# A loading stage reordered, a PSUM place alternated and DMA transposes moved to mid-batch in an attention and gated-FFN kernel

## The chip, the cores and the metric

The kernel runs on one core of a Trainium2 chip. The metric is the device time of one execution in microseconds; a profiled span is about 1.8 us shorter than the time of the same execution. In this text PE is TensorE, DVE is VectorE, ACT is ScalarE, POOL is GpSimd and SP is the engine whose queue issues most DMAs (72 of the 86 issues that the old kernel's DMA view lists). "Granted clock" is the TensorE clock that the profile records as granted, as a share of full speed.

Ratios are computed as the mean time of one kernel's fast runs over the mean of the other kernel's fast runs in the same rounds, so they are not quite the ratio of the medians quoted beside them. Each experiment was timed against the old kernel in the same rounds; medians of different groups of rounds differ by up to 1.4 us for the old kernel itself (259.6 to 261.0), so across groups the ratios are the better guide.

## The reference

For each of 8 batches and 8 heads, a cross attention in both directions between x (512 rows of 64) and a state (32 rows of 64); then a gated feed-forward layer over all rows.

```python
scores = scale * x @ state^T;  a  = softmax(scores);  xread = a @ state      # 512 rows per head
scores2 = scale * state @ x^T; a2 = softmax(scores2); sread = a2 @ x         # 32 rows per head
t = concat(xread, sread) over rows, heads side by side                        # (8 * 544, 512)
out = (sigmoid(t @ w_gate) * (t @ w_val)) @ w_out                             # d_ff = 1536
```

## The kernel before

PSUM holds the buffers that this kernel's matmuls write to; an eviction is the copy of a result out of such a buffer, here by ACT or DVE (a 128x512 copy of SW took 0.59 us on ACT and 0.68 us on DVE in the old kernel).

The kernel never forms xread. It multiplies the state with the gate and value weights first (SW, "visits"), and the attention a^T (aT) is then the moving operand of the gate/value matmuls. For one batch there are 12 gate/value steps `gv`, each four 128x512 matmuls, then 12 output steps `out_mm` of four. Batch b's output steps run one batch behind, woven into batch b+1's loop, together with the attention of the batch after that (nb).

```python
def at_xT_dma(b):                       # x^T by four DMA transposes on SP's queue
    for c in range(4):
        nc.sync.dma_start_transpose(xT[:, :, c], xbs[b][:, c]...)

def at_S(b, i, place):                  # scores, then E = exp on ACT
    for jj in range(2):
        for c in range(4):
            nc.tensor.matmul(ps[...], xTs[b][:, 2*i+jj, c], sTz[:, b, 2*i+jj], ...)
    nc.scalar.activation(E1s[b]..., ps..., AF.Exp, scale=scale)

def at_norm(b, i, eng):                 # rs = row sums, ri = 1/rs, ab = E * ri
    nc.vector.tensor_reduce(rs, E, AX.X, ALU.add)
    nc.vector.reciprocal(ri, rs)
    eng.tensor_tensor(abs_[b]..., E, ri.unsqueeze(3).to_broadcast(...), ALU.mult)

def gv(b, f, place=None):               # two PSUM buffers, one tanh on ACT, one multiply on DVE
    # (four matmuls, cut)
    nc.scalar.activation(th, pss[0], AF.Tanh, scale=0.5)
    nc.vector.scalar_tensor_tensor(glus[b][:, f], th, 1.0, pss[1], ALU.add, ALU.mult)

def out_mm(b, k):                       # row block c = k // 3, a third of its 12 matmuls
    if f0 == 0:
        ops[b, c] = p_out.tile(...) if b < B else p_sw.tile(...)   # p_out holds ONE buffer
    # (four matmuls; after the last third: copy by ACT, then the store on SP's queue)
```

The loading order: state and x of batch 0 on SP's queue; on POOL's queue the first 256 columns of both weights, x of batch 1, the rest of the weights, x of batch 2, and later w_out. The loop, cut to what the argument needs:

```python
for b in range(1, B + 1):
    for f in range(12):
        out_mm(b - 1, f)                          # for b > 1 also gv(b, f)
        if f == 0:
            if b > 1: at_xT_dma(nb)               # transposes of nb = b + 1
            load_x(nb + 1, nc.sync)
        elif f == 2: at_S(nb, 0, AT)              # needs the transposes
        elif f == 3: at_S(nb, 1, AT)              # AT: one PSUM buffer
        elif f == 4: at_norm(nb, 0, nc.vector); at_Eb(nb)   # Eb: casts of E on POOL
        elif f == 5: at_norm(nb, 1, nc.vector)
        elif f == 7: at_aT(nb, AT, (vec,))
        elif f == 8: at_sr(nb, AT)
        if f == 11: cast_x(nb + 1, pool, 0, 4); cast_x(nb + 1, pool, 4, 4)
```

The softmax here doesn't subtract the row's maximum and nothing guards it: scores larger than these inputs give would overflow.

## Time and profile before

The old kernel takes 260.53 us (median of 4 runs, 259.14 to 261.48). Three markers in the trace cut its span into stages: the first output matmul, the first gate/value step of batch 2, and the last output copy of batch 6.

| stage | from, us | to, us | length, us |
|---|---|---|---|
| loading, batches 0 and 1 | 0 | 57.75 | 57.75 |
| batch 1 of the loop (output of batch 0) | 57.75 | 75.25 | 17.50 |
| batches 2 to 6 | 75.25 | 205.73 | 130.48 |
| the rest | 205.73 | 257.9 | 52.17 |

The page of the old kernel has the span in 40 slices of 6.4 us; each digit is a share in tenths, PE's busy share and then its granted clock.

```profile
span 257.9 us, 4608 instructions
...
PE   7677499899887999899989998999899999999994
...
PEclk9959769999999999999999999999999999999999
```

PE looks busy nearly everywhere, but the clock falls to 5, 7 and 6 tenths in slices of the loading stage. The timeline of the old kernel's PE shows what goes before the last of these falls. The columns are start, length, what, and in brackets the idle time before it and what ended it.

```profile
26.57 0.62 PE L171 MATMUL swp<-wv,sTz 64*32 64x512 bf16 x8
29.82 1.03 PE L139 MATMUL aTp<-ident,ab 128*128 128x128 bf16 x8 [2.64 <-DVE ab L132]
32.03 4.36 PE L207 MATMUL gvp<-aT,SW 128*128 128x512 bf16 x10 [1.18 <-DVE aT L143]
```

After 2.64 us of idleness the eight small transposes take 1.03 us, and ten gate/value matmuls take 4.36 us, some 430 ns each against 216 at a full clock (0.86 us from one step of four to the next, 77.64 to 78.50 to 79.36 us). The granted clock was 0.50 from 30 to 35 us.

The waits of the old kernel's PE over the whole span (total, times, longest):

```profile
PE Sp L115 <- DMA xT<-xb: 5.5, 7, 1.1
PE aTp L139 <- DVE ab L132: 2.6, 1, 2.6
PE outp L228 <- ACT res L232: 1.9, 3, 0.7
```

The chain that ended last, on the page, by engine and by line:

```profile
PE 58%; DVE 11%; SPq 9%; DMA 7%; ACT 6%; issue 5%; POOL 1%; ACTq 0%; DVEq 0%; POOLq 0%
PE outp L228 24%; PE gvp L207 22%; SPq L107 8%; DMA xT<-xb 5%; DVE glu L215 4%; PE gvp L210 4%; PE swp L171 3%; ACT th L214 2%; DVE rs L129 2%; ACT res L232 2%; DMA xf<-in_x_dram 2%; PE Sp L115 2%; PE aTp L139 1%; PE srp L152 1%; ACT SW L193 1%
```

The issue of the transposes (L107) and their flight (xT) are on the chain with 13%. That is not what can be saved: during most of it PE has other work. The saving is what PE waits, and the timeline of batch 2 shows it:

```profile
74.88 5.97 SPq L107 DMA_TRANSPOSE xT<-xb  x4
...
80.23 0.22 PE L115 MATMUL Sp<-sTz,xT 128*128 128x64 bf16 x2
...
80.81 0.20 PE L115 MATMUL Sp<-sTz,xT 128*128 128x64 bf16 x1 [0.37 <-DMA xT<-xb]
...
82.12 0.32 PE L115 MATMUL Sp<-sTz,xT 128*128 128x64 bf16 x5 [1.11 <-DMA xT<-xb]
82.28 1.03 PE L228 MATMUL outp<-wo,glu 128*128 128x512 bf16 x4
```

The four transposes occupy SP's queue for 5.97 us from step 0 on, each lands 2.5 us after its issue (median of the 24 in the trace, 2.4 to 6.0), and PE arrives at the scores of step 2 after 5.35 us. Eight score matmuls that wait for nothing take 0.23 us (the next eight, at 84.17, in the chain); here the next output matmul starts 2.05 us after the first of the eight.

### The profile page before, as it was taken

What the parts mean: (1) busy time and instruction counts of PE and PEld (TensorE: products, weight loads), DVE (VectorE), ACT (ScalarE), POOL (GpSimd) and SP (SyncE); (2) the same over time, 40 slices, a digit from 0 to 9 for tenths busy, and PEclk for the clock granted to TensorE, in tenths of its full rate; (3) what the DMA queues carried; (4) which work ended last, traced back from release to release, by engine and by line L of the source; (5) the groups of instructions that cost most, each with busy time, mean ns of one, the idle gap of its engine ahead of it and who ended that gap; (6) DMA issues with size and microseconds to landing.
All of it is one profiled execution on the core that took longest, in us unless ns stands there. A gap on an engine that the chain in (4) does not pass through costs nothing.

```text
span 257.9 us, 4608 instructions
## 1 busy us (share of the span) xinstructions
PE 232.3 (90%) x1816; PEld 116.0 (45%) x1816; DVE 120.5 (47%) x201; ACT 140.8 (55%) x262; POOL 41.1 (16%) x71
## 2 busy tenths in 40 slices
PE   7677499899887999899989998999899999999994
PEld 7434233343433454444434443444344544466643
DVE  3714945773332664376535653565337543332210
ACT  3557347675645756675567556765556554433311
POOL 4974220000500600050005000500020000000000
PEclk9959769999999999999999999999999999999999
DMA  7999999001144511551165105610511111111103
GB/s 236 180 234 206 283 189 226 3 0 43 41 103 100 206 43 56 103 211 41 39 100 194 68 22 128 192 66 21 119 41 42 43 66 56 43 41 57 67 21 101
DMA packets 30965, 25.98 MB, mean 101 GB/s; under 512 B 14048, under 2 KB 26080, under 8 KB 30944
## 3 DMA queue, kind: packets, MB, share of 16 engines
q1 hardware_dynamic: 24448, 18.75, 25.6%
q0 software_dynamic: 6352, 6.82, 14.1%
q8 instruction: 14, 0.23, 0.3%
q10 hardware_dynamic: 144, 0.13, 0.1%
q14 instruction: 7, 0.06, 0.1%
HBM read 18.35 MB, written 8.91 MB: 106 GB/s over the span
## 4 chain that ended last, share of the span: by engine, by line
PE 58%; DVE 11%; SPq 9%; DMA 7%; ACT 6%; issue 5%; POOL 1%; ACTq 0%; DVEq 0%; POOLq 0%
PE outp L228 24%; PE gvp L207 22%; SPq L107 8%; DMA xT<-xb 5%; DVE glu L215 4%; PE gvp L210 4%; PE swp L171 3%; ACT th L214 2%; DVE rs L129 2%; ACT res L232 2%; DMA xf<-in_x_dram 2%; PE Sp L115 2%; PE aTp L139 1%; PE srp L152 1%; ACT SW L193 1%
## 5 line engine op out<-in xcount | busy, mean ns | idle before, releaser
L215 DVE SCALAR_TENSOR_TENSOR glu<-th,gvp 128x512 bf16<-128x512 f32 (+1 forms) x108 | 70.9, 658 | 105.5 <-ACT th L214 73.8
L207 PE MATMUL gvp<-aT,SW 128*128 128x512 bf16 x384 | 100.9, 389 | 5.8 <-DVE aT L143 1.7
L228 PE MATMUL outp<-wo,glu 128*128 128x512 bf16 x396 | 100.3, 379 | 1.9 <-ACT res L232 1.9
L214 ACT ACTIVATE th<-gvp 128x512 f32<-128x512 f32 (+1 forms) x108 | 61.8, 573 | 65.2 <-PE gvp L207 54.3
L207 PEld LDWEIGHTS <-SW 128*128 128x128 bf16 x384 | 38.1, 100 | 54.7 <-issue 13.0
L228 PEld LDWEIGHTS <-glu 128*128 128x128 bf16 x396 | 36.3, 98 | 43.5 <-issue 7.4
L193 ACT CAST SW<-swp 128x512 bf16<-128x512 f32 x92 | 52.5, 588 | 6.2 <-PE swp L171 5.4
L122 POOL CAST Eb<-E 128x256 bf16<-128x256 f32 x32 | 11.9, 415 | 140.4 <-ACT E L116 140.4
L232 ACT ACTIVATE res<-outp 128x512 f32<-128x512 f32 x33 | 19.7, 597 | 26.5 <-PE outp L228 24.1
L86 POOL CAST xb<-xf 128x1024 bf16<-128x1024 f32 x14 | 16.0, 1172 | 7.2 <-DMA xf<-in_x_dram 6.5
L116 ACT ACTIVATE E<-Sp 128x512 f32<-128x512 f32 x16 | 9.6, 608 | 6.4 <-PE Sp L115 6.4
L115 PE MATMUL Sp<-sTz,xT 128*128 128x64 bf16 x128 | 7.5, 194 | 6.2 <-DMA xT<-xb 5.5
L171 PE MATMUL swp<-wv,sTz 64*32 64x512 bf16 (+1 forms) x208 | 11.0, 365 | 2.2 <-DMA wv<-in_moe_w_val_dram 1.5
L129 DVE TENSOR_REDUCE rs<-E 128x16 f32<-128x512 f32 x16 | 10.9, 679 | 4.2 <-ACT E L116 4.2
L132 DVE TENSOR_TENSOR ab<-E,ri 128x512 bf16<-128x512 f32 x15 | 11.6, 774 | 0.5
L115 PEld LDWEIGHTS <-xT 128*128 128x128 bf16 x128 | 6.1, 98 | 10.5 <-DMA xT<-xb 6.3
L171 PEld LDWEIGHTS <-sTz 64*32 64x32 bf16 x416 | 4.4, 89 | 13.2 <-issue 12.4
L171 PE MATMUL swp<-wg,sTz 64*32 64x512 bf16 (+1 forms) x208 | 10.1, 370 | 0.0
L158 DVE RECIPROCAL r<-srp 128x128 f32<-128x128 f32 x8 | 7.7, 956 | 4.9 <-PE srp L155 4.9
L139 PE MATMUL aTp<-ident,ab 128*128 128x128 bf16 x64 | 5.7, 241 | 3.5 <-DVE ab L132 2.6
L263 PE MATMUL warm<-ident 128*128 128x128 bf16 x68 | 6.9, 280 | 1.4 <-POOL ident masks.py:199 1.4
L143 DVE COPY aT<-aTp 128x1024 bf16<-128x1024 bf16 (+1 forms) x8 | 5.2, 653 | 5.5 <-PE aTp L139 5.5
(47 smaller groups left out, 102.5 us busy)
## 6 DMA issues: line engine op xcount, KB each, us to landing
out_dram<-res SPq DMA_DIRECT2D x31, 256.0 KB, 2.3
xf<-in_x_dram SPq DMA_DIRECT2D x5, 1024.0 KB, 5.9
xf<-in_x_dram POOLq DMA_DIRECT2D x2, 1024.0 KB, 14.1
wo<-in_moe_w_out_dram POOLq DMA_DIRECT2D x3, 512.0 KB, 16.2
xf<-in_x_dram SPq DMA_DIRECT2D x2, 512.0 KB, 5.1
wg<-in_moe_w_gate_dram POOLq DMA_DIRECT2D x2, 512.0 KB, 13.5
wv<-in_moe_w_val_dram POOLq DMA_DIRECT2D x2, 512.0 KB, 15.3
sf<-in_state_dram SPq DMA_DIRECT2D x1, 512.0 KB, 3.6
```

The lines of the kernel that those rows point to most:

```text
L86: cp(xbs[b].rearrange("p c h d -> p h c d")[:, lo:lo + n], xfs[b][:, lo:lo + n])
L107: nc.sync.dma_start_transpose(xT[:, :, c], xbs[b][:, c].rearrange("p h d -> p (h d)"))
L115: nc.tensor.matmul(ps[:, c, :, jj], xTs[b][:, 2 * i + jj, c], sTz[:, b, 2 * i + jj], start=True, stop=True)
L122: nc.gpsimd.tensor_copy(Ebs[b][:, c], E1s[b][:, c])
L129: nc.vector.tensor_reduce(rs, E, AX.X, ALU.add)
L171: nc.tensor.matmul(pss[e][j * Ns:(j + 1) * Ns, o:o + n], sTz[rows, b, j, e], (wg, wv)[w][rows, j, lo:lo + n], start=True, stop=True)
L193: cp(*sw_left.pop(0))
L207: nc.tensor.matmul(ps, SWs[b][:, g, w, fs], aTs[b][:, g], start=(g == 0), stop=(g == 1))
L214: nc.scalar.activation(th, pss[0], AF.Tanh, scale=0.5)
L215: nc.vector.scalar_tensor_tensor(glus[b][:, f], th, 1.0, pss[1], ALU.add, ALU.mult)
L228: nc.tensor.matmul(ops[b, c], glus[b][:, f, c * 128:(c + 1) * 128], wo[:, f], start=(f == 0), stop=(f == NF - 1))
L232: nc.scalar.activation(res, ops[b, c], AF.Copy, scale=0.5)
```

## The change

The intent: x of batches 0 and 1 ahead of all weights, so that both attentions are done by the time the first weights land; then one list of gate/value steps and visits, with evictions shared evenly between ACT and DVE; two PSUM places for the row blocks of batch 0's output; and in the loop the casts of x at step 5 and the transposes at step 7, for the next batch but one, in place of step 11 and step 0. The diff, cut to its core:

```diff
 def out_mm(b, k):
-            ops[b, c] = (p_out.tile(...) if b < B else p_sw.tile(...))
+            place = SWP if b == B else GV if b == 0 and c % 2 else OU
+            ops[b, c] = place[0].tile((128, 512), FP, name="outp", tag=place[1])
 ...
     load_x(0, nc.sync, 2)
+    load_x(1, nc.sync)
 ...
-    load_w(0, 256)
-    load_x(1, nc.gpsimd)
-    load_w(256, 256)
-    load_w(512, 512)
-    ...                                  # attention 0, then gv, visits and attention 1 mixed by hand
+    at_xT_pe(0, 0, AT, (vec,))           # attention 0
+    ...
+    load_w(0, 256)
+    ...
+    at_norm(0, 1, nc.vector)
+    load_w(256, 256)
+    cast_x(1, pool, 4, 4)
+    ...                                  # other weights, x of batch 2, w_out
+    warm(32, SWP)                        # 32 dummy matmuls
+    at_xT_pe(1, 0, OU, (act,))           # attention 1
+    at_aT(0, AT, (vec, act))
+    at_xT_pe(1, 1, OU, (vec,))
+    warm(8, SWP)
+    ...                                  # first visit, scores of batch 1, gv(0, 0), gv(0, 1)
+    sT_copy(0, slice(2, B), act)         # transposed state of batches 2 to 7, on ACT
+    at_norm(1, 0, nc.vector)
+    sT_copy(1, slice(2, B), act)
+    at_norm(1, 1, nc.vector)
+    order = [(sw_visit, 1, 0, 256), (sw_visit, 0, 256, 256), (gv, 0, 2), (at_aT, 1, AT, (vec,)), (gv, 0, 3), ...]
+    for fn, *args in order:
+        ...
+        fn(*args)
+        sw_evac(act, vec)
 ...
                 if f == 0:
-                    if b > 1:
-                        at_xT_dma(nb)
                     if nb + 1 < B:
                         load_x(nb + 1, nc.sync)
 ...
                 elif f == 5:
                     at_norm(nb, 1, nc.vector)
+                    if nb + 1 < B:
+                        cast_x(nb + 1, pool, 0, 4)
+                        cast_x(nb + 1, pool, 4, 4)
                 elif f == 7:
                     at_aT(nb, AT, (vec,))
+                    if nb + 1 < B:
+                        at_xT_dma(nb + 1)
 ...
-                if nb + 1 < B and f == 11:
-                    cast_x(nb + 1, pool, 0, 4)
-                    cast_x(nb + 1, pool, 4, 4)
```

More of the change, by code (lines that the diff above doesn't have):

```diff
@@ L60 @@
     XS = wp.tile((128, 4, B * Ns), BF, name="XS")
+    AT, OU, GV, SWP = (p_at, "at"), (p_out, "outp"), (p_gv, "gv"), (p_sw, "swp")
     xfs, xbs, xTs = {}, {}, {}
@@ L172, in sw_mm, with sw_visit @@
                                  (wg, wv)[w][rows, j, lo:lo + n], start=True, stop=True)
-    def sw_visit(b, lo, n):
+    def sw_visit(b, lo, n, *ws):
         if b not in SWs:
             SWs[b] = fp.tile((128, 2, 2, dff), BF, name="SW", bufs=2)
-        if n == 256:
+        if not ws:
             pss = [p_sw.tile((128, 512), FP, name="swp", tag="swp") for e in range(2)]
@@ L182, in sw_visit @@
                 sw_left.append((SWs[b][:, e, :, lo:lo + n], pss[e].rearrange("p (w n) -> p w n", w=2)))
-        else:
-            for w in range(2):
-                pss = [p_sw.tile((128, 512), FP, name="swp", tag="swp") for e in range(2)]
-                sw_mm(pss, b, w, lo, n, 0)
-                for e in range(2):
-                    sw_left.append((SWs[b][:, e, w, lo:lo + n], pss[e]))
+        for w in ws:
+            pss = [p_sw.tile((128, 512), FP, name="swp", tag="swp")[:, :n] for e in range(2)]
+            sw_mm(pss, b, w, lo, n, 0)
+            for e in range(2):
+                sw_left.append((SWs[b][:, e, w, lo:lo + n], pss[e]))
     def sw_evac(*cps):
@@ L224, in out_mm @@
         if f0 == 0:
-            ops[b, c] = (p_out.tile((128, 512), FP, name="outp", tag="outp") if b < B
-                         else p_sw.tile((128, 512), FP, name="outp", tag="swp"))
+            place = SWP if b == B else GV if b == 0 and c % 2 else OU
+            ops[b, c] = place[0].tile((128, 512), FP, name="outp", tag=place[1])
         for f in range(f0, f0 + 4):
@@ L254, in out_last, with warm @@
                 nc.sync.dma_start(rows_of(b, c)[:, cs], res[:, cs])
-    AT, OU, GV, SWP = (p_at, "at"), (p_out, "outp"), (p_gv, "gv"), (p_sw, "swp")
-    def warm(n):
-        ps = p_gv.tile((128, 512), FP, name="warm", tag="gv")
+    def warm(n, place):
+        ps = place[0].tile((128, 512), FP, name="warm", tag=place[1])
         for _ in range(n):
@@ L274 @@
     nc.scalar.activation(pre, ident[:, 0:1], AF.Exp)
-    warm(36)
+    warm(36, SWP)
     sb = wp.tile((128, 16, 2, D), BF, name="sb")
     nc.vector.tensor_copy(sb[:, :, 0], sf)
-    nc.scalar.copy(sb[:, 0:12, 1], sf[:, 0:12])
-    nc.gpsimd.tensor_copy(sb[:, 12:16, 1], sf[:, 12:16])
-    load_w(0, 256)
-    load_x(1, nc.gpsimd)
-    load_w(256, 256)
-    load_w(512, 512)
-    load_w(1024, 512)
-    load_x(2, nc.gpsimd)
-    cast_x(0, vec, 0, 4)
+    nc.scalar.copy(sb[:, :, 1], sf)
+    cast_x(0, vec, 0, 2)
+    cast_x(0, act, 2, 2)
     stp = []
     for i in range(2):
-        ps = p_sw.tile((128, 8, 128), BF, name="stp", tag="swp")
+        ps = p_gv.tile((128, 8, 128), BF, name="stp", tag="gv")
         for l in range(8):
@@ L302, in sT_copy @@
             cp(dst, src.rearrange("p b j u l -> p (b j) u l"))
-    sT_copy(0, slice(0, 1), vec)
-    sT_copy(1, slice(0, 1), act)
     at_xT_pe(0, 0, AT, (vec,))
+    sT_copy(0, slice(0, 2), vec)
+    sT_copy(1, slice(0, 2), act)
+    cast_x(0, pool, 6, 2)
     cast_x(0, act, 4, 2)
-    cast_x(0, vec, 6, 2)
-    warm(8)
+    load_w(0, 256)
+    warm(4, SWP)
     at_S(0, 0, OU)
-    at_xT_pe(0, 1, AT, (vec,))
-    at_norm(0, 0, nc.gpsimd)
-    warm(8)
-    at_S(0, 1, GV)
-    sT_copy(0, slice(1, B), act)
@@ L316 @@
-    at_norm(0, 1, nc.vector)
-    warm(8)
-    sw_visit(0, 0, 256)
-    sw_evac(act, act)
-    warm(8)
-    at_aT(0, AT, (vec, act))
-    sT_copy(1, slice(1, B), act)
-    cast_x(1, pool, 0, 4)
+    at_xT_pe(0, 1, SWP, (vec, act))
+    at_norm(0, 0, nc.vector)
+    at_S(0, 1, SWP)
+    cast_x(1, act, 0, 4)
+    at_norm(0, 1, nc.vector)
+    load_w(256, 256)
     cast_x(1, pool, 4, 4)
-    at_Eb(0)
+    load_w(512, 512)
+    load_w(1024, 512)
+    load_x(2, nc.gpsimd)
     for q in range(3):
         load_wo(q)
-    gv(0, 0)
@@ L331 @@
-    gv(0, 1, SWP)
-    at_xT_pe(1, 0, AT, (vec,))
-    at_xT_pe(1, 1, OU, (act,))
-    sw_visit(0, 256, 256)
-    sw_evac(act, vec)
-    sw_visit(1, 0, 256)
-    gv(0, 2)
-    sw_evac(act, act)
-    at_S(1, 0, AT)
-    at_S(1, 1, OU)
-    gv(0, 3, SWP)
-    sw_visit(1, 256, 256)
+    warm(32, SWP)
[3 more added lines that the diff above has]
+    warm(8, SWP)
+    sw_visit(0, 0, 256, 0)
+    sw_evac(act, vec)
+    at_S(1, 0, AT)
+    sw_visit(0, 0, 256, 1)
@@ L343 @@
+    sw_evac(act, vec)
+    gv(0, 0, SWP)
+    at_S(1, 1, OU)
+    gv(0, 1, SWP)
+    sT_copy(0, slice(2, B), act)
     at_norm(1, 0, nc.vector)
+    sT_copy(1, slice(2, B), act)
     at_norm(1, 1, nc.vector)
+    at_Eb(0)
     at_Eb(1)
-    sw_evac(act, act)
-    at_sr(0, OU)
-    sw_visit(0, 512, 512)
-    sw_evac(act, act, act)
-    at_aT(1, AT, (vec,))
-    sw_evac(vec)
-    gv(1, 0)
-    gv(1, 1, SWP)
-    gv(0, 4)
-    gv(1, 2, SWP)
-    sw_visit(1, 512, 512)
-    sw_evac(act, act)
-    gv(1, 3)
@@ L359 @@
-    sw_evac(act, act)
-    gv(0, 5, SWP)
-    gv(0, 6)
-    gv(1, 4, SWP)
-    gv(1, 5)
-    gv(0, 7, SWP)
-    sw_visit(0, 1024, 512)
-    sw_evac(act, vec)
-    gv(1, 6)
-    sw_evac(act, act)
-    gv(1, 7, SWP)
-    at_sr(1, OU)
-    gv(0, 8)
-    sw_visit(1, 1024, 512)
-    sw_evac(act, vec)
-    gv(0, 9, SWP)
-    sw_evac(act, act)
+    order = [(sw_visit, 1, 0, 256), (sw_visit, 0, 256, 256), (gv, 0, 2), (at_aT, 1, AT, (vec,)), (gv, 0, 3),
+             (sw_visit, 1, 256, 256), (gv, 1, 0), (gv, 1, 1), (gv, 1, 2),
+             (sw_visit, 0, 512, 512, 0), (gv, 1, 3), (sw_visit, 0, 512, 512, 1), (at_sr, 0, OU), (gv, 0, 4),
+             (sw_visit, 1, 512, 512, 0), (gv, 0, 5), (sw_visit, 1, 512, 512, 1), (gv, 0, 6), (gv, 0, 7), (gv, 1, 4),
+             (gv, 1, 5), (sw_visit, 0, 1024, 512, 0), (gv, 1, 6), (sw_visit, 0, 1024, 512, 1), (gv, 1, 7),
+             (at_sr, 1, OU), (gv, 0, 8), (sw_visit, 1, 1024, 512, 0), (gv, 0, 9), (sw_visit, 1, 1024, 512, 1),
+             (gv, 0, 10), (gv, 0, 11), (gv, 1, 8), (gv, 1, 9), (gv, 1, 10), (gv, 1, 11)]
@@ L376 @@
+    n_gv = 0
+    for fn, *args in order:
+        if fn is gv:
+            args.append(SWP if n_gv % 2 else GV)
+            n_gv += 1
+        fn(*args)
+        sw_evac(act, vec)
     cast_x(2, pool, 0, 4)
@@ L378 @@
     at_xT_dma(2)
-    gv(0, 10)
-    gv(0, 11, SWP)
-    for f in range(8, NF):
-        gv(1, f, SWP if f % 2 else GV)
     for b in range(1, B + 1):
@@ L393 @@
                 if f % 4 == 0:
-                    sw_visit(nb, f * 128, 512)
+                    sw_visit(nb, f * 128, 512, 0, 1)
                 sw_evac(act)
                 if f == 0:
-                    if b > 1:
-                        at_xT_dma(nb)
                     if nb + 1 < B:
```

## The prediction

> **What bounds the kernel now** (chain of waits, timeline, windows).
>
> 1. Loading, 0 to 57.8 us (first output matmul at 57.75). The stage holds 24 gate/value steps of four 128x512 matmuls. A step takes 0.86 us when nothing waits, so they need 20.7 us; from the first at 16.1 us they take 41.7. TensorE's granted clock is 0.59 at 15 to 20 us and 0.50 at 30 to 35 us, after idle stretches (2.6 us at 29.8 before the transpose of batch 1's attention). Eight matmuls there take 3.44 us, 430 ns each, against 216 warm. [...] ACT carries most evictions (0.59 us per 128x512), in clumps, while DVE idles.
> 2. Batch 1 of the loop, 57.8 to 74.4 us: one output PSUM buffer, so the next row block waits for ACT's copy. Waits: 1.9 us in three, plus drains, about 2.3 us.
> 3. Batches 2 to 6, periods 25.8 to 26.7 us: DMA transposes are issued at step 0 (four of 1.2 to 2.1 us on the queue, then 2.5 us to landing), and scores need them at step 2. Waits charge 5.5 us to this; from the score matmuls' ideal end to the next output matmul I count 1.8, 0.9, 1.3, 0.9 and 1.9: 6.8 us.
> 4. After 206 us all is PE-bound at 1.73 us per pair, and unchanged.
>
> **What changes.**
> - Stage 3: casts at step 5, transposes at step 7, some 8 us before their use. All 6.8 us lie on the critical path. In the old trace the casts already run at steps 4 to 5 (87.07 us), because POOL waits for x, so no new collision with DVE. I allow 0.5 us for new waits: gain 6.3 us.
> - Stage 2: output blocks alternate two pools: gain 2.3 us.
> - Stage 1: x of batch 1 puts about 3 us of DMA (x of batch 0 landed 2.9 us after state) ahead of the first weights, whose issue also moves from 5.3 to about 8 us. Both attentions fill that gap, with dummy matmuls keeping the clock. First gate/value step at 16 to 17.5 us, no earlier than now. After it DVE owes 24 x 0.69 + 11 evictions x 0.68 + normalisation of batch 1 3.3 + state read 3.1 + one copy 0.7, or 31 us; ACT about 24; PE about 26. DVE becomes the limit. At 88% use (guess) the stage ends 35 us later, near 52 us: gain about 5.5 us, the least certain term. The last weight chunk should land near 32 us and be needed near 38.
>
> Sum: 14.1 us. I take 13.4, allowing for small new waits: 260.4 - 13.4 = 247.0 us, 243 to 252.
>
> **What would show it.** First output matmul at 50 to 54 us; granted clock at least 0.95 from 16 us on; DVE over 80% busy from 17 to 50 us. No PE wait on the DMA transpose, periods of batches 2 to 6 near 24.9 us. No wait of output matmuls on ACT's copy in batch 1, which lasts about 14.2 us.
>
> **What would make it wrong.** Weights landing later than 15.5 us, or a chunk arriving after its visit (waits on weight DMA); TensorE falling cold again; DVE's order stalling PE in the loading stage (gate/value matmuls waiting on DVE), leaving its end near 55 us; transposes holding the issue queue at step 7 and delaying output stores; with the transpose wait gone, gate/value steps waiting for DVE at steps 4 to 6, 0.5 us or more per batch.
>
> Chances: faster by over 2% 0.92, within 2% 0.07, slower 0.01.

## The result

The new kernel takes 247.88 us (median of 4 runs, 247.49 to 248.67). The ratio to the old one is 0.9522, with a 95% interval of 0.9473 to 0.9572.

| stage | before, us | after, us | gain, us | predicted gain, us |
|---|---|---|---|---|
| loading | 57.75 | 53.01 | 4.74 | 5.5 |
| batch 1 | 17.50 | 15.76 | 1.74 | 2.3 |
| batches 2 to 6 | 130.48 | 125.11 | 5.37 | 6.3 |
| the rest | 52.17 | 52.22 | -0.05 | 0 |

The markers after are 53.01, 68.77, 193.88 and 246.1 us. The gains of the two profiles add up to 11.8 us, where the medians differ by 12.65; the experiment on the loading stage shows where the rest probably lies. The page of the new kernel, slices of 6.2 us:

```profile
span 246.1 us, 4632 instructions
...
PE   7674999999999999999999999999999999999993
...
PEclk9998699999999999999999999999999999999999
```

One deep dent of the clock is left (8 and 6 tenths, 18 to 31 us). The chain that ended last has no transposes on it any more:

```profile
PE 76%; DVE 13%; issue 4%; ACT 4%; DMA 2%; SPq 0%; ACTq 0%; DVEq 0%
```

The longest waits of the new kernel's PE, and the one that is new in batch 1:

```profile
PE gvp L208 <- DVE glu L216: 2.5, 9, 0.3
PE gvp L208 <- ACT SW L194: 2.0, 2, 1.8
PE gvp L208 <- DVE SW L194: 1.6, 1, 1.6
...
PE Sp L116 <- ACT E L117: 0.6, 1, 0.6
```

The waits for the transposes (5.5 us) and for ACT's output copy (1.9 us) are gone. The last line came in their place. In batch 1 the steps are short, because there are no gate/value steps yet. The second score matmuls now arrive before ACT has emptied the one buffer that both use.

The transposes of batch 4, in the new kernel's timeline:

```profile
80.62 5.12 SPq L108 DMA_TRANSPOSE xT<-xb  x4
...
99.18 0.40 PE L116 MATMUL Sp<-sTz,xT 128*128 128x64 bf16 x8
99.42 1.03 PE L229 MATMUL outp<-wo,glu 128*128 128x512 bf16 x4
```

They are issued 18.6 us before the scores that use them; the eight score matmuls run together, and the output matmul follows 0.24 us after their start (2.05 us in batch 2 before).

The loading stage is less clean. In the new kernel's timeline between 19 and 29 us, ACT and DVE have older work in front of the evictions (SW) that the third gate/value step waits for:

```profile
19.57 1.92 ACT L296 COPY sTz<-stp 64x384 bf16<-64x384 bf16 x4
...
22.64 0.61 PE L208 MATMUL gvp<-aT,SW 128*128 128x512 bf16 x1 [1.78 <-ACT SW L194]
...
23.54 1.28 DVE L194 CAST SW<-swp 128x512 bf16<-128x512 f32 x2
24.88 1.46 PE L208 MATMUL gvp<-aT,SW 128*128 128x512 bf16 x3 [1.62 <-DVE SW L194]
...
26.98 1.91 PE L208 MATMUL gvp<-aT,SW 128*128 128x512 bf16 x4
```

The windows view of the same stretch (window and length, busy us and number of instructions of each engine, granted clock, DMA share, GB/s):

```profile
20.00:25.00 5.00, 1.14 (x17) 0.37 (x17) 4.68 (x9) 2.53 (x6) 2.27 (x6) 0.74 1.24 207
25.00:30.00 5.00, 5.00 (x34) 2.07 (x34) 2.37 (x4) 1.71 (x4) 0.00 (x0) 0.58 1.13 301
```

PE worked 1.14 of 5 us, the clock fell (0.74, then 0.58), and the next four matmuls took 1.91 us in place of 1.03.

### The profile page after: what moved, and what is told of

Read it like the earlier page. It is cut to its first block, busy times and chain, and to the rows that moved or that the text cites. A ratio compares the mean times of both kernels' runs of the same rounds, so it can differ in the third digit from the quotient of the medians.

```text
span 246.1 us, 4632 instructions
## 1 busy us (share of the span) xinstructions
PE 229.8 (93%) x1828; PEld 114.4 (46%) x1828; DVE 128.4 (52%) x210; ACT 139.2 (57%) x258; POOL 36.4 (15%) x68
## 4 chain that ended last, share of the span: by engine, by line
PE 76%; DVE 13%; issue 4%; ACT 4%; DMA 2%; SPq 0%; ACTq 0%; DVEq 0%
PE outp L229 30%; PE gvp L208 29%; PE swp L172 5%; DVE glu L216 4%; PE gvp L211 4%; DVE rs L130 3%; DVE ab L133 3%; PE srp L153 2%; PE aTp L140 2%; ACT th L215 2%; DMA sf<-in_state_dram 2%; PE srp L156 2%; DVE ri L132 1%; PE Sp L116 1%; ACT E L117 1%
## 5 line engine op out<-in xcount | busy, mean ns | idle before, releaser
L208 PEld LDWEIGHTS <-SW 128*128 128x128 bf16 x384 | 36.7, 98 | 53.1 <-issue 7.9
L194 ACT CAST SW<-swp 128x512 bf16<-128x512 f32 (+1 forms) x85 | 48.7, 581 | 7.9 <-PE swp L172 7.1
L87 POOL CAST xb<-xf 128x1024 bf16<-128x1024 f32 (+1 forms) x14 | 14.3, 1045 | 19.0 <-PE srp L156 13.0
L133 DVE TENSOR_TENSOR ab<-E,ri 128x512 bf16<-128x512 f32 x16 | 15.8, 989 | 0.5
L172 PE MATMUL swp<-wg,sTz 64*32 64x512 bf16 (+1 forms) x208 | 10.6, 374 | 0.5 <-DVE glu L216 0.5
L116 PE MATMUL Sp<-sTz,xT 128*128 128x64 bf16 x128 | 6.5, 193 | 2.5 <-DVE sTz L296 1.1
L194 DVE CAST SW<-swp 128x512 bf16<-128x512 f32 (+1 forms) x13 | 8.3, 643 | 0.3 <-PE swp L172 0.2
L211 PE MATMUL gvp<-XS,wv 128*128 128x256 bf16 x48 | 7.2, 272 | 0.1
## 6 DMA issues: line engine op xcount, KB each, us to landing
wv<-in_moe_w_val_dram POOLq DMA_DIRECT2D x2, 512.0 KB, 11.8
```

The costliest lines, as they stand in the source:

```text
L87: cp(xbs[b].rearrange("p c h d -> p h c d")[:, lo:lo + n], xfs[b][:, lo:lo + n])
L116: nc.tensor.matmul(ps[:, c, :, jj], xTs[b][:, 2 * i + jj, c], sTz[:, b, 2 * i + jj], start=True, stop=True)
L133: eng.tensor_tensor(abs_[b].rearrange("p c e (j n) -> p (c e) j n", n=Ns)[:, :, 2 * i:2 * i + 2], E, ri.unsqueeze(3).to_broadcast((128, 8, ...
L172: nc.tensor.matmul(pss[e][j * Ns:(j + 1) * Ns, o:o + n], sTz[rows, b, j, e], (wg, wv)[w][rows, j, lo:lo + n], start=True, stop=True)
L194: cp(*sw_left.pop(0))
L208: nc.tensor.matmul(ps, SWs[b][:, g, w, fs], aTs[b][:, g], start=(g == 0), stop=(g == 1))
```

## The experiments

Twelve kernels were run, all with correct results, each in five rounds. By the record's rule (2%) three are called unclear: the loading stage alone, the loop part alone and the late issue. Their intervals lie wholly below 1 but reach across 0.98. The parts of the change were first taken alone, on the old kernel.

### The loading stage alone

The edit: the new kernel with the old loop and the old PSUM place.

```diff
-place = SWP if b == B else GV if b == 0 and c % 2 else OU
+place = SWP if b == B else OU
 ...           # casts back to step 11, transposes back to step 0
```

> The old kernel with the new loading stage alone (old loop, old PSUM place of the output blocks). My theory: the three parts of the change act in separate stages and add up, so this one gives the 4.7 us by which the first output matmul moved (57.75 to 53.01): about 255.8 us, first output matmul near 53.0, batches 2 to 6 as in the old kernel, with waits on the DMA transposes of about 5.5 us. Rival: the parts overlap (an earlier end of loading meets transposes that are not ready, or the loop's gain needs the new loading); then this gives under 3 or over 7 us.

Measured: 255.21 us against 259.59, ratio 0.9797 (0.9749 to 0.9846), which is 5.3 us (0.0203 of 260). The stages add up as expected here. The size carries noise: the six runs span 252.77 to 256.36 us. Five profiles have the same new loading code (the new kernel, this one, and below the early casts, the late issue and the PSUM place taken out); the first output matmul is recorded at 53.01, 52.84, 54.29, 53.70 and 53.55 us. Three have the old one (the old kernel, and below the PSUM place alone and the loop part alone): 57.75, 58.93 and 59.36. The 4.74 us of the table above are therefore a single reading of a stage that moves by 1.5 us by itself; the two means, 53.5 and 58.7, differ by 5.2 us, which fits this experiment.

### The PSUM place alone

```diff
-ops[b, c] = (p_out.tile(...) if b < B else p_sw.tile(...))
+place = SWP if b == B else GV if b == 0 and c % 2 else OU
```

> The old kernel with the alternating PSUM place of batch 0's output blocks alone. Theory: the three waits of output matmuls on ACT's copy (1.9 us) and their drains go, 2.3 us in all, but 0.6 us comes back as a wait of the second score matmuls on the eviction of the first, because they share one PSUM buffer and the steps are now shorter: net 1.7 us, about 258.8 us. Rival: no wait comes back in this kernel, and the net is 2.3 us; or it is lost at the transposes that follow, and the net is 0.

Measured: 261.25 us against 259.59, ratio 1.0051 (1.0007 to 1.0095). My 258.8 was wrong; the rival that the time is lost at the transposes holds. The expected wait on ACT's E (0.6 us) is there and the output waits are gone, and batch 1 takes 15.76 us (58.93 to 74.69) in place of 17.50. But the interval from the last output copy of batch 0 to that of batch 1 is 28.64 us (74.08 to 102.72) where the old kernel has 26.71. The timeline of this kernel at step 2 of batch 2:

```profile
75.21 5.97 SPq L107 DMA_TRANSPOSE xT<-xb  x4
...
79.67 0.42 PE L115 MATMUL Sp<-sTz,xT 128*128 128x64 bf16 x2
81.14 0.20 PE L115 MATMUL Sp<-sTz,xT 128*128 128x64 bf16 x1 [1.05 <-DMA xT<-xb]
...
82.47 0.45 PE L115 MATMUL Sp<-sTz,xT 128*128 128x64 bf16 x5 [1.13 <-DMA xT<-xb]
82.73 1.89 PE L228 MATMUL outp<-wo,glu 128*128 128x512 bf16 x4
```

PE now reaches the scores 4.46 us after the first transpose was issued, not 5.35, so it waits 2.2 us there in place of 1.5. And four output matmuls take 1.89 us in place of 1.03: the clock has fallen. The windows confirm it (0.57 against 1.00), this kernel first, then the old one:

```profile
82.00:86.00 4.00, 3.53 (x18) 1.52 (x18) 0.00 (x0) 1.08 (x2) 0.00 (x0) 0.57 0.70 212
```

```profile
82.00:86.00 4.00, 3.88 (x29) 1.86 (x29) 0.69 (x1) 2.44 (x5) 0.52 (x2) 1.00 0.85 266
```

In this run, what was saved before the transposes was paid back at them, with the cold clock on top. The dip is read from one profiled run, the slowest of the six. The six runs have a granted clock of 0.966 to 0.974 over the span, ten of the eleven old ones 0.980; that fits such a dip in all of them but doesn't say where it lies.

### The PSUM place taken out of the new kernel

```diff
-place = SWP if b == B else GV if b == 0 and c % 2 else OU
+place = SWP if b == B else OU
```

> The new kernel with the alternating PSUM place put back to one buffer. Theory: in the old loop the time that this part saves was given back two steps later, at the transposes (alone it gave 1.005 of the old time, with waits on the transposes of 6.3 us); with the transposes early nothing waits there, so the part keeps its 1.7 us: this kernel should take about 249.6 us (ratio 0.959), with 1.9 us of waits of output matmuls on ACT's copy, and no wait on transposes. Rival: the part is worth nothing in either kernel (then 247.9 us, ratio 0.952), and the 4 us by which the three parts alone fall short of the whole come from elsewhere.

Measured: 249.71 us against 259.77, ratio 0.9603 (0.9558 to 0.9647), as expected to 0.1 us. In its profile the 1.9 us of waits on ACT's copy are back and there is none on transposes. So the same edit is worth about 0.8% in the new kernel (0.9522 over 0.9603; the two intervals just overlap) and nothing or less in the old one. The profile gives the same size: batch 1 takes 17.50 us again (53.55 to 71.05) in place of 15.76, and batches 2 to 6 take 125.15 us as in the new kernel. This also explains why the parts don't multiply to the whole: 0.9797 x 1.0051 x 0.9829 (the last from the next experiment) is 0.968, not 0.952. Without the PSUM part they do: 0.9797 x 0.9829 is 0.963, and the kernel that has both measured 0.9603.

### The casts and transposes alone, and the transposes' issue alone

The first edit puts the two hunks of the loop into the old kernel. The second takes the new kernel and puts back only the issue:

```diff
                 if f == 0:
+                    if b > 1:
+                        at_xT_dma(nb)
 ...
-                    if nb + 1 < B:
-                        at_xT_dma(nb + 1)
```

> The old kernel with casts at step 5 and transposes at step 7 alone. Theory: the wait of score matmuls on the DMA transpose goes in batches 2 to 6, about 6.3 us net: 254.2 us; periods between the last output copies of successive batches from 26.4 to about 25.1 us, with the batches in which the cast of x meets DVE's normalisation near 25.4 and the one without a cast near 24.9. Rival: the loop's gain in the full change came from elsewhere (clock, loading), and this gives under 4 us.

> The new kernel with one thing put back: transposes issued at step 0 of the next batch, casts still at step 5. Theory: the issue position alone made the wait (the old casts already ran at steps 4 to 5), so all the loop's gain goes again: about 6 us lost, near 254 us, waits of score matmuls on the transposes of 5 us or more. Rival: the earlier casts carry a part, and then under 4 us is lost.

Measured, the loop part alone: 255.56 us against 259.59, ratio 0.9829 (0.9792 to 0.9866), 4.4 us. That is less than the 6.3 us expected; by the interval it is 3.5 to 5.4 us, so the time alone doesn't exclude the rival (under 4), and the trace has to. In its trace the waits on transposes are gone. From the first gate/value step of batch 2 to the last copy of batch 6 it takes 125.20 us (76.86 to 202.06), like the new kernel (125.11) and 5.3 us less than the old one. The 1.0 us missing from my 6.3 is put down to the collision of casts and normalisation that the experiment with early casts measures below. The further 0.9 us between 5.3 and 4.4 lies within the scatter of the loading stage, whose first output matmul is recorded at 59.36 us here with unchanged code (57.75 in the old kernel's profile).

Measured, the issue put back: 255.0 us, ratio 0.9818 (0.9779 to 0.9857), 7.1 us slower than the new kernel by the medians and 7.7 us by the ratios, with 6.0 us of waits on transposes, though the casts are as early as in the new kernel. The issue position alone makes the wait; the rival, that the early casts carry a part, falls.

### x of batch 1 first, alone

```diff
     load_x(0, nc.sync, 2)
+    load_x(1, nc.sync)
 ...
     load_w(0, 256)
-    load_x(1, nc.gpsimd)
```

> The old kernel with one load moved: x of batch 1 is issued right behind x of batch 0, ahead of all weights, and nothing else. Theory: the load order alone gains nothing, because the old order does not look at batch 1 before its first two gate/value steps, and the first weights come some 2 to 3 us later: first gate/value step near 17.5 us instead of 16.1, time from unchanged to 1.5 us longer (260 to 262 us). Rival: the early x is what ends the loading stage sooner, through an earlier cast on POOL: then about 256 us.

Measured: ratio of the fast runs 1.0007 (0.9939 to 1.0075); the median of all six, 262.74 us, includes three that count as slow, and the profiled run was one of those, so its trace is not used to explain a time. The load order that heads the description of the change shows no gain by itself (the interval leaves room for 0.6%); the gain of the loading stage needs the new order of the work that uses it. Which part of that order gives it (the early attention of batch 1, the even evictions, the new list) was not taken apart.

### The dummy matmuls taken out

```diff
-    warm(32, SWP)
-    warm(8, SWP)
```

> The new kernel without the 40 dummy matmuls (32 and 8) of the loading stage. Theory: they keep the granted clock at 1.0 through 20 us; without them TensorE is idle for most of 10.7 to 14.6 us, the clock falls to half somewhere in 11 to 20 us, but the matmuls there are few and wait on other engines, so under 1 us is lost: 248 to 249 us. Rival: the cold clock carries into the gate/value steps and costs 2 us or more.

Measured: 248.33 us, ratio 0.9512 (0.948 to 0.9545): the same as the new kernel. The clock falls to 0.61 at 10 to 15 us and 0.71 at 15 to 20, as expected, and nothing is lost. That fits the expected reason, that PE waits on other engines there anyway (1.6 us for the cast of x on ACT and 1.1 us for the multiply on DVE). These dummies keep a clock that nothing needs.

### The casts of x ahead of the casts of E

In the new kernel, POOL's cast of x runs while DVE multiplies E by ri. Two lines of its batch 3:

```profile
104.00 2.02 POOL L87 CAST xb<-xf 128x1024 bf16<-128x1024 f32 x2
105.11 1.45 DVE L133 TENSOR_TENSOR ab<-E,ri 128x512 bf16<-128x512 f32 x1
```

The multiply takes 1.45 us where it takes 0.69 alone (at 105.86 us in the kernel with early casts below). The casts stood beside the multiply in the old kernel too, as in its batch 2:

```profile
87.07 2.49 POOL L86 CAST xb<-xf 128x1024 bf16<-128x1024 f32 x2 [0.15 <-POOL Eb L122]
87.97 0.69 DVE L132 TENSOR_TENSOR ab<-E,ri 128x512 bf16<-128x512 f32 x1
```

The difference is which begins first. In the old kernel's batches 2, 4 and 5 the multiply began 0.09 to 0.18 us before the second of the two casts, and that cast took 1.50 us in place of 1.04. In its batch 3, and in batches 2 to 5 of the new kernel, the second cast began 0.05 to 0.13 us before the multiply, and the multiply took 1.45 to 1.54 us. The delay then reaches PE through DVE's queue: over batches 2 to 6 gate/value matmuls wait 2.5 us for the multiply of their step (glu), and 1.1 us in the kernel with early casts below. The interval between the last output copies is 25.43 to 25.44 us in three of the batches with a cast, and 24.90 us in the one without (168.98 to 193.88). The edit:

```diff
                 elif f == 2:
                     at_S(nb, 0, AT)
+                    if nb + 1 < B:
+                        cast_x(nb + 1, pool, 0, 4)
+                        cast_x(nb + 1, pool, 4, 4)
 ...
-                    if nb + 1 < B:
-                        cast_x(nb + 1, pool, 0, 4)
-                        cast_x(nb + 1, pool, 4, 4)
```

> The new kernel with the casts of x moved from step 5 to step 2, ahead of the casts of E on POOL; transposes stay at step 7. Theory: in batches 2 to 5 the cast of x runs beside DVE's normalising multiply, which then takes 1.45 us instead of 0.69, and this is why those periods are 25.43 us while the batch without a cast has 24.90. With the cast done before the multiply, all periods go to about 24.9 us: 2.1 us saved, about 245.8 us. Rival: the slow multiply is absorbed and the batch without a cast is shorter for another reason (no transposes or x load in it): no gain, 247.9 us. Second rival: x lands too late for step 2, the casts of E wait behind it, and the state read at step 8 stalls.

Measured: 246.65 us against 261.03, ratio 0.9437 (0.9402 to 0.9473), 2.2 us better than 0.9522 of 260. The same batch in its timeline:

```profile
101.48 2.02 POOL L87 CAST xb<-xf 128x1024 bf16<-128x1024 f32 x2 [20.62 <-issue]
103.45 1.43 POOL L123 CAST Eb<-E 128x256 bf16<-128x256 f32 x4
105.86 0.69 DVE L133 TENSOR_TENSOR ab<-E,ri 128x512 bf16<-128x512 f32 x1
```

The intervals are 23.99, 24.91, 24.91, 24.90 and 24.91 us, 123.62 in sum in place of 125.72: the 2.1 us expected. Why cast and multiply slow each other was not shown; the traces give the times, 1.45 us against 0.69.

One more such pair was not tested by itself. In the new loading stage the first multiply of batch 0 takes 2.18 us (from 10.77) while POOL casts x of batch 1 (11.31 to 12.40), and it lies on the chain that leads to the first gate/value step. (It takes 1.36 us in the last kernel below.)

### The hole of the loading stage

The hole is the stretch from 20.9 to 24.9 us in which PE has almost nothing to do. Two edits on the new kernel; the second contains the first.

```diff
     cast_x(1, act, 0, 4)
+    sT_copy(0, slice(2, B), act)
 ...
     at_xT_pe(1, 0, OU, (act,))
+    sT_copy(1, slice(2, B), act)
 ...
-    sT_copy(0, slice(2, B), act)
-    sT_copy(1, slice(2, B), act)      # end of the first edit
-    at_norm(1, 0, nc.vector)
-    at_norm(1, 1, nc.vector)
-    order = [..., (sw_visit, 0, 256, 256), (gv, 0, 2), (at_aT, 1, AT, (vec,)), (gv, 0, 3), ...
+    order = [..., (sw_visit, 0, 256, 256), (at_norm, 1, 0, nc.vector), (gv, 0, 2),
+             (at_norm, 1, 1, nc.vector), (gv, 0, 3), (at_aT, 1, AT, (vec,)), ...
```

> The new kernel with the four copies of the transposed state for batches 2 to 7 (1.92 us on ACT) moved into ACT's idle time before 15.7 us. Theory: in the loading stage TensorE idles from 20.9 to 24.9 us because both ACT (state copies) and DVE (normalisation of batch 1, 3.3 us) have older work queued in front of the two evictions that the third gate/value step needs; DVE is the later one. So this alone gives at most 0.5 us, about 247.5 us, and the third step still starts its second half near 24.9. Rival: ACT is what held it, and 2 to 3 us are gained.

> As the state-copies kernel, and batch 1's normalisation is also put behind the evictions on DVE. Theory: the third gate/value step starts near 21.8 us instead of 24.9, the clock stays up through 30 us, and about 2.5 to 3.5 us are saved: 244.4 to 245.4 us. Rival: the stage is limited by weights still arriving; then waits on the weight DMA appear and the first output matmul stays near 53 us. Second rival: the wait moves to the transpose of batch 1's attention, which now comes later, the clock falls there, and under 1 us is saved.

Measured, the copies alone: 248.36 us, ratio 0.9514 (0.9481 to 0.9548), no gain. The wait on ACT's eviction shrank from 1.8 us to 0.7, and the wait on DVE's grew from 1.6 us to 3.0. DVE held the step, as expected; two queues stood in the way, and clearing one showed nothing.

Measured, both: 246.45 us, ratio 0.9436 (0.9397 to 0.9476), about 2.2 us better than the new kernel by the ratios, a little under the 2.5 to 3.5 us that I expected. The six runs span 245.14 to 247.84 us, and their granted clocks over the span tell which is which: 1.0 and 0.999 in the two fastest (245.22 and 245.14), 0.992 to 0.993 in the three between, 0.986 in the slowest. The profiled run is that slowest one:

```profile
26.21 0.62 PE L140 MATMUL aTp<-ident,ab 128*128 128x128 bf16 x8 [2.05 <-DVE ab L133]
...
27.61 4.45 PE L208 MATMUL gvp<-aT,SW 128*128 128x512 bf16 x12 [0.45 <-DVE aT L144]
```

The third gate/value step starts at 22.26 us, but the wait has moved to the transpose of batch 1's attention, as the second rival said. In this run the clock fell behind it (1.00 at 24 to 26 us, 0.50 at 28 to 30 and 0.67 at 30 to 32): twelve matmuls take 4.45 us, 2.76 in the new kernel at that place. No wait on the weights' DMA appears, so the first rival falls.

### Evictions moved from DVE to ACT

```diff
-        sw_evac(act, vec)
+        sw_evac(act, act if fn is sw_visit and args[2:] == [512, 1] else vec)
```

> The new kernel with four of DVE's eight evictions of the late 512-wide visits in the loading stage moved to ACT (2.7 us off DVE, 2.4 us onto ACT). Theory: from 30 to 53 us DVE is the limit (93% busy there), TensorE alone would need about 21.6 of 23.7 us; so the first output matmul comes about 1 us earlier and the time falls by 0.5 to 1.5 us, to 246.4 to 247.4. Rival: TensorE's own order is the limit there, and nothing is gained or ACT's clumps lose 0.5 us or more.

Measured: 248.49 us, ratio 0.9556 (0.9514 to 0.9599); no gain. DVE's busy time between the first gate/value step and the first output matmul fell from 28.88 us (of 36.10) to 26.5 and the stage did not shorten beyond its scatter. The rival holds: from 30 us on DVE is busy (20.43 of 23 us, 89% and not the 93% of my expectation) but not the limit. The new kernel's chain of waits, asked for 30 to 53 us alone, has nothing but PE on it, and the waits view records no wait of PE there. With the evictions moved, ACT and DVE come onto that chain with 12%. What keeps PE at 23.7 us from the first gate/value step of batch 1 (29.34) to the first output matmul, where a sum of its work in that stretch gives an estimate of 21.6 (20 steps of 0.865, eight half visits of 0.28, two state reads of 1.02), is not settled. Eight matmuls of a visit take 0.73 us in some places and 0.41 in others (at 33.34 and 32.04 us in the new kernel); the cause was not tested.

### All findings together

The casts at step 2, the two edits on the hole, the first multiply of batch 1's normalisation on POOL, the evictions of the experiment above, and:

```diff
-             (sw_visit, 1, 256, 256), (gv, 1, 0), ...
+             (gv, 0, 3), (sw_visit, 1, 256, 256), (warm, 24, SWP), (at_aT, 1, AT, (vec,)), (gv, 1, 0), ...
-                    at_S(nb, 1, AT)
+                    at_S(nb, 1, GV if b == 1 else AT)
```

> All findings together, on the new kernel: casts of x at step 2; state copies in ACT's idle time; batch 1's normalisation behind the evictions, its first multiply on POOL; the visit of batch 1 and 24 dummy matmuls in front of the transpose of batch 1's attention to keep the clock; four evictions moved to ACT; the second score matmuls of batch 2 in another PSUM buffer. Theory: 2.1 us from the casts, 2 to 3 us from the loading stage, 0.6 us from the score buffer: 242.5 to 244 us, with the granted clock above 0.9 from 16 us on. Rival: the loading stage only shifts its wait again (as the copies-and-normalisation kernel did in its profiled run), and only the casts' 2.1 us and the score buffer's 0.6 remain: about 245.2 us.

Measured: 243.11 us against 259.77, ratio 0.9352 (0.9309 to 0.9395), within the expected range and faster than both kernels. The clock's line on the page of this kernel, and its windows where the new kernel has 0.74 and 0.58:

```profile
PEclk9999999999999999999999999999999999999999
```

```profile
20.00:25.00 5.00, 3.81 (x61) 2.33 (x62) 4.59 (x9) 2.78 (x5) 2.61 (x6) 1.00 1.24 207
25.00:30.00 5.00, 3.83 (x33) 1.78 (x31) 3.34 (x7) 1.79 (x3) 0.00 (x0) 1.00 1.14 301
```

The clock stays full (1.00 in both windows). The first output matmul comes at 51.19 us, and the first gate/value step of batch 2 follows 15.07 us later (15.76 in the new kernel). The six runs lie between 243.06 and 243.32 us, a tenth of the scatter of the copies-and-normalisation kernel. In the copies-and-normalisation kernel the scatter went with the clock, as its six runs show. For the others the clock is not all of it: with one and the same granted clock, 0.986, runs of the early casts span 245.58 to 246.93 us. Which share of the stage's gain belongs to the dummies, to the multiply on POOL and to the order was not separated.

## Why the prediction was right

The time was right: 247.0 us predicted, 247.88 measured, in the range of 243 to 252, and faster by over 2% as the most likely case. The mechanisms of two stages were right and each stage's gain was forecast somewhat too large; the allowance of 0.7 us on the sum took up a part of that, and the loading stage came out near for other reasons than those given (point 7), which is luck. Point by point:

1. **"Stage 3 ... gain 6.3 us."** The mechanism was shown: the wait is gone, putting back the issue alone brings it back, and the early casts don't matter for it. The size was 5.4 us. The 6.8 us of waits were well counted: with the early casts the same stage takes 123.01 us (70.05 to 193.06), 7.5 less than in the old kernel, and part of that is the old kernel's own collision. The mis-sized term is the 0.5 us allowed for new waits, see the next point. The transposes were issued further ahead than the forecast 8 us (18.6 in batch 4 above).
2. **"so no new collision with DVE."** This step failed. In the old trace the casts did run at steps 4 to 5, but in three batches of four the multiply began first and the cast took the delay (multiply 0.69 to 0.78 us, once 1.54). In the new one the casts follow the casts of E at once, the second begins 0.13 us before the multiply, and the multiply takes 1.45 us in each of batches 2 to 5. The prediction's own list of what would make it wrong had this: "gate/value steps waiting for DVE at steps 4 to 6, 0.5 us or more per batch". The experiment with early casts put this at 2.1 us over four batches, some 0.5 us each. The old kernel pays that in one batch only (1.54 us at 113.76), so about 1.6 us were new, where I had allowed 0.5; 6.8 less 1.6 is 5.2.
3. **"periods of batches 2 to 6 near 24.9 us."** Measured 25.43 in three of the batches with a cast and 24.90 in the one without. The figure did not follow from my own sum either: 6.3 us over five batches is 1.26 each, from 26.4 to 25.1, and 25.1 is the measured mean.
4. **"Stage 2: output blocks alternate two pools: gain 2.3 us."** 1.74 us. The term missing was the 0.6 us wait of the second score matmuls on ACT, which shorter steps expose. The forecast length of 14.2 us missed by more: to the marker that the prediction used, the end of batch 0's last copy, the stage takes 15.75 us after 16.59 before, because the third of the three waits is for that very copy and delays only what follows it. Not foreseen: this gain exists only with the early transposes; alone it was given back there.
5. **"First gate/value step at 16 to 17.5 us"** and **"First output matmul at 50 to 54 us"** were right: 16.93 and 53.01.
6. **"granted clock at least 0.95 from 16 us on"** failed: 0.74 at 20 to 25 us and 0.58 at 25 to 30. I had read the idle stretches of the old order and assumed that the new order had none. It has one, because ACT and DVE carry older work in front of two evictions.
7. **"DVE becomes the limit. At 88% use (guess) the stage ends 35 us later, near 52 us"** failed as a mechanism though its end was near. DVE was busy 80% of that time (28.88 of 36.10 us), but taking 2.4 us off it gained nothing. The stage is made of a hole with a cold clock up to 29 us, and after it a stretch in which PE waits for no engine and its own order is the limit as far as the traces show.

## What to carry to other kernels

A saving can be lost again at a later wait: here the same PSUM edit was worth about 2 us with the transposes early and nothing with them late, so measure parts both alone and taken out of the whole. When an engine waits for two others, look at both queues for older work before moving either. A scatter of one per cent between runs of one kernel is worth a look at the granted clock of each run: the six runs of the copies-and-normalisation kernel (245.14 to 247.84 us) went with clocks of 1.0 to 0.986, and the last kernel, whose clock stayed at 0.998 to 1.0, was both faster and steadier (243.06 to 243.32 us).
